# Attention with a gated memory part, ahead of two mixture stages: the memory's normalisation moved into column layout

## Chip, cores and metric

The kernel runs on one core of one Trainium2 chip. The metric is the device time of one execution in microseconds (us); times are compared as the median of several runs. TensorE multiplies matrices into PSUM banks, VectorE (DVE), ScalarE (ACT) and GpSimd (POOL) work elementwise, and SyncE (SP) issues most transfers.

## What is computed

The change lies in the first stage, an attention over 4 x 8 heads of 576 tokens and 64 features. Its output is a gated sum of a causal softmax attention and of a lookup in a memory matrix, which is divided by a norm. Two mixture stages follow, which the change doesn't touch.

```python
def _attn_ref(q, k, v, M_prev, z_prev, beta):
    scores = scale * np.matmul(q, k.transpose(0, 1, 3, 2))   # causal mask, softmax -> a
    local = np.matmul(a, v)
    def phi(x):
        return np.where(x > 0, x, np.exp(x) - 1.0) + 1.0
    q_p = phi(q)
    mem_ret = np.einsum('bhsd,bhde->bhse', q_p, M_prev)
    mem_norm = np.einsum('bhsd,bhd->bhs', q_p, z_prev)[..., None] + 1e-06
    mem_out = mem_ret / mem_norm
    g = 1.0 / (1.0 + np.exp(-beta))[None, :, None, None]
    return g * mem_out + (1 - g) * local
```

All of it is in float32. The host lays q and k out with features on partitions, two heads (a pair) stacked to 128 partitions; M of a pair is block diagonal, 128 x 128, and the two columns behind it hold z, each in its head's rows.

## The kernel before

The order of the work on every engine is the order in which the code is written; the tools add the waits. There are 16 pairs of heads (n), and each has four units (u): the first covers 256 query tokens, two cover 128 each, the last covers 64. The main loop runs over the 64 units, t = 4n + u. In step t it issues, in this order: the scores of unit t+3 (`scores`, L311 and L318, for a last unit L340 and L341), the rest of the softmax of unit t+1, the product with the values of unit t-1 (`av`, L399 and L404), the transposes of unit t (`transp`, L364, for a last unit L372 and L374), the exponentials of unit t+3, and what `later` has booked for step t (`run_late`). `scores` leaves a row maximum from DVE (L322, L343), exponentials from ACT (L327, L345), and on POOL a multiplication by the reciprocal of the sum and by 1-g (L337, L351); the reciprocals are DVE's (L331, L349). The transposed probabilities go from PSUM to SBUF on ACT and DVE (L367, L369).

The memory part is `phi_part`, a generator that is advanced one piece at a time. For pair m the pieces are booked in the steps of the pair before it: in the first step ACT's exponential of q (L267) and POOL's gate on M (L268; L270 copies the two z columns behind it into the same tile mg); in the second DVE's features (L272, L273, tile phi, two buffers); in the third and fourth the lookup. There TensorE takes 128 tokens of the features as weights and moves mg with its 130 columns (L279, three matmuls, then two), with tokens on partitions in `bank[6]`; DVE adds 1e-6 to the two norm columns, takes the reciprocal (L282, L283) and multiplies the rest by it into mem (L284). In `av` that result is brought into column layout, with features on partitions, by a matmul with mem as weights and the identity as the moving operand (L404), which adds to the sums of L399 in `bank[7]`. ACT copies them to xT (L85, `put_x`).

During the attention DVE, ACT and POOL also convert weights of the first mixture stage (`convert`, L237 to L246, transfers L221 and L224, the tile cst), and in steps 39 to 60 split its first inputs (L448 on DVE, L449 on POOL). For the loads of later pairs SP waits until the buffer of two pairs before is read: qr and mr (M and z) have two buffers each.

Of the kernel before, what the change touches and what calls it, by code (L numbers as in the profile page):

```python
# [9 lines left out]
F32 = mybir.dt.float32  # L10
# [7 lines left out]
ALU = mybir.AluOpType  # L18
# [3 lines left out]
P = 128  # L22
# [9 lines left out]
def kernel(ctx, tc, qt, kt, vt, mt, beta, w_in, w_out,  # L32
                           w_gate, w_noise, noise, w1, w2, out):

    nc = tc.nc
    NPAIR, _, S = kt.shape
    H, D = beta.shape[0], 64
    B = 2 * NPAIR // H
    NT = B * S
    NB = (S + P - 1) // P  # L40
    TAIL = S - (NB - 1) * P
    HS = S // 2
    QW, MW = qt.shape[-1], mt.shape[-1]
# [8 lines left out]
    bank = [two[i // 2][:, i % 2, :] for i in range(4)] + [psp.tile([P, 512], F32, name=f"bk{i}") for i in range(4, 8)]  # L52
# [7 lines left out]
    ident = const.tile([P, P], F32, name="ident")  # L60
# [48 lines left out]
    def consts():  # L109
        nc.gpsimd.memset(padr, 0.0)  # L110
        nc.gpsimd.iota(padr[:, :, P], pattern=[[P, CAP // P]], base=NT, channel_multiplier=1,
                       allow_small_or_imprecise_dtypes=True)
        yield
        nc.gpsimd.memset(tri, 1.0)
        nc.gpsimd.affine_select(out=tri, in_=tri, pattern=[[1, P]], compare_op=ALU.is_gt,
                                fill=0.0, base=0, channel_multiplier=-1)
        nc.gpsimd.memset(onesb, 1.0)
        yield
        for t, pat, m in ((iota8, [[1, NE]], 0), (runs, [[STRIDE, NE]], 0), (pid, [[0, 1]], 1), (tokid, [[P, NOISE_T]], 1)):
            nc.gpsimd.iota(t, pattern=pat, base=0, channel_multiplier=m, allow_small_or_imprecise_dtypes=True)  # L120
        yield
        nc.gpsimd.memset(wgt, 0.0)
        for j, src in enumerate((w_gate, w_noise)):
            nc.sync.dma_start(wgt[:, :, j * NE:(j + 1) * NE], _ap(src, 0, [[NE, P], [P * NE, NCC], [1, NE]]))
        nc.sync.dma_start(noise_sb, _ap(noise, 0, [[NE, P], [P * NE, NOISE_T], [1, NE]]))
        yield
# [123 lines left out]
        i = 4 * fc + 2 * which  # L250
        return U[i], U[i + 1]

    qs, mem, mg, PB, PT = {}, {}, {}, {}, {}

    def scaled(n):

# [3 lines left out]
    def phi_part(n):  # L260

        qq = qr_[n % 2][:, :S]
        e = ap2.tile([P, S], F32, name="phe", bufs=1)
        ph = ap2.tile([P, S], F32, name="phi", bufs=2)
        mg = ap2.tile([P, MW], F32, name="mg", bufs=1)
        mem[n] = ap2.tile([P, NB, P], F32, name="mem")
        nc.scalar.activation(e, qq, AF.Exp)  # L267
        nc.gpsimd.tensor_scalar(mg[:, :P], mr_[n % 2][:, :P], gtc[:, n % (H // 2):n % (H // 2) + 1], 1.0,  # L268
                                op0=ALU.mult, op1=ALU.mult)
        nc.gpsimd.tensor_copy(mg[:, P:], mr_[n % 2][:, P:])  # L270
        yield
        nc.vector.tensor_scalar_min(e, e, 1.0)  # L272
        nc.vector.scalar_tensor_tensor(ph, qq, 0.0, e, op0=ALU.max, op1=ALU.add)  # L273
        yield
        for ts in ((0, 1, 2), (3, 4)):
            k_ = len(ts)
            for i, t in enumerate(ts):
                w = min(P, S - t * P)
                nc.tensor.matmul(bank[6][:w, i * MW:(i + 1) * MW], ph[:, t * P:t * P + w], mg, start=True, stop=True)  # L279
            r = bank[6][:, :k_ * MW].rearrange("p (t c) -> p t c", c=MW)  # L280
            rd = ap2.tile([P, 3, 2], F32, name="rd")[:, :k_, :]
            nc.vector.tensor_scalar_add(rd, r[:, :, P:], 1e-6)  # L282
            nc.vector.reciprocal(rd, rd)  # L283
            nc.vector.tensor_tensor(mem[n][:, ts[0]:ts[0] + k_, :].rearrange("p t (j d) -> p t j d", j=2),  # L284
                                    r[:, :, :P].rearrange("p t (j d) -> p t j d", j=2),
                                    rd[:, :, :, None].to_broadcast([P, k_, 2, D]), op=ALU.mult)
            yield

    LEAD = 3
# [64 lines left out]
    def transp(t):  # L354
        n, u = units[t]
        pb = PB.pop(t)
        pt = ap3.tile([P, 2 * 512], F32, name="PT", bufs=2)
        PT[t] = pt
        if u < NK - 1:
            m = sum(w for _, w, _ in tiles(u))  # L360
            blocks = [(0, 0), (1, 1), (2, 2)] if u == 0 else [(c, c) for c in range(u + 2)]
            for j in range(2):
                for c, x in blocks:
                    nc.tensor.transpose(bank[4 + j][:, x * P:(x + 1) * P], pb[:, j * 512 + c * P:j * 512 + (c + 1) * P], ident)  # L364
                dst = pt[:, j * 512:j * 512 + m]
                if j == 0:
                    nc.scalar.activation(dst, bank[4][:, :m], AF.Copy)  # L367
                else:
                    nc.vector.tensor_copy(dst, bank[5][:, :m])  # L369
        else:  # L370
            for c in range(4):
                nc.tensor.transpose(bank[4][:, c * P:(c + 1) * P], pb[:, c * P:(c + 1) * P], ident)  # L372
            nc.scalar.activation(pt[:, :512], bank[4], AF.Copy)
            nc.tensor.transpose(bank[5][:TAIL, :P], pb[:, 4 * P:S], ident)  # L374
            nc.vector.tensor_copy(pt[:TAIL, 512:512 + P], bank[5][:TAIL, :P])

    def av(t):
        n, u = units[t]
        b, hp = n // (H // 2), n % (H // 2)
        vv = vr_[n % 2].rearrange("p (c j d) -> p c j d", c=NB, j=2)  # L380
        pt = PT.pop(t)
        q0 = (u + 1) * P if u else 0
        if u == 0:
            w = 2 * P
            work = [(0, P, 0, 0, w), (1, P, w, P, w)]
            rows = [(0, 0), (1, P)]
        elif u < NK - 1:
            w = P
            work = [(c, P, c * P, 0, w) for c in range(u + 2)]
            rows = [(u + 1, 0)]  # L390
        else:
            w = TAIL
            work = [(c, P, c * P, 0, w) for c in range(4)] + [(4, TAIL, 512, 0, w)]
            rows = [(u + 1, 0)]
        o = bank[7][:, :w]
        step = TAIL if u == NK - 1 else 512
        for i, (c, k_, x, a, e) in enumerate(work):
            for j in range(2):
                nc.tensor.matmul(o[j * D:(j + 1) * D, a:e], vv[:k_, c, j, :], pt[:k_, j * step + x:j * step + x + e - a],  # L399
                                 start=i == 0, stop=False, skip_group_check=True)  # L400
        for i, (qi, a) in enumerate(rows):
            k_ = min(P, w)
            for j in range(2):
                nc.tensor.matmul(o[j * D:(j + 1) * D, a:a + k_], mem[n][:k_, qi, j * D:(j + 1) * D], ident[:k_, :k_],  # L404
                                 start=False, stop=i + 1 == len(rows), skip_group_check=True)
        put_x(hp, b * S + q0, o)

    NU = len(units)
    CONV0, CONVR, CONVM = 3, 4.1, 1.9
    late = {}  # L410

    def later(step, gen):
        late.setdefault(max(step, -1), []).append(gen)
# [5 lines left out]
    for m in range(1, NPAIR):  # L419
        later(NK * (m - 1) - 1, first(m))  # L420
        gen = phi_part(m)
        for k_ in range(4):
            later(NK * (m - 1) + k_, gen)
    gen = consts()
    for k_ in range(4):
        later(k_, gen)
# [64 lines left out]
    for t in range(NU):  # L491
        n, j = divmod(t, NK)
        ahead = t + LEAD < NU
        if ahead:
            sg[t + LEAD] = scores(t + LEAD)
            next(sg[t + LEAD])
            next(sg[t + LEAD])
        for _ in sg.pop(t + 1, ()):
            pass
        if t:  # L500
            av(t - 1)
        else:
            next(phi0)
        transp(t)
        if t + 2 in sg:
            next(sg[t + 2])
        for g in range(2):
            cs = [c for c in range(NCC) if early[g][c] == t]
            if cs:
                hb = p1(g, 0, g, cs)  # L510
            if NCC - 1 in cs:
                act = act1(hb, True)
                ahead_of[g] = next(act)
                next(act)
        if ahead:
            next(sg[t + LEAD])
        if not t:
            next(phi0)
        run_late(t)
        d, m = divmod(t - 39, 3)  # L520
        if m == 0 and 0 <= d < 2 * NCC:
            split_x(d // NCC, d % NCC, nc.gpsimd, nc.vector.tensor_copy)
        if j == 0:
            next(fill, None)
        if j == 1 and n + 1 < NPAIR and n:
            load(n + 1, (vr_,))
        if j == 0 and not n:
            load(2, (qr_, mr_))
        if j == 2:
            if n + 2 < NPAIR:  # L530
                load(n + 2, (kr_,))
            if n + 3 < NPAIR:
                load(n + 3, (qr_, mr_))
# [539 lines left out]
```

## Time and profile before

| | |
|---|---|
| median of 3 runs | 1130.9 us (1129.4 to 1130.94) |
| profiled execution | 1130.14 us, span 1128.4 us |
| TensorE matmul busy | 1101.8 us (98%), 7182 instructions |
| weight loads busy | 956.0 us (85%) |
| DVE, ACT, POOL busy | 590.6, 513.3, 241.1 us |

The page divides the span into 40 slices of 28.2 us; the attention takes a little over the first eight. TensorE's busy time is modelled from pipelined instructions, and a full row does not mean that the array moves columns all the time. The weight loads (PEld) run beside the matmuls, in the same order, and their start times tell when the engine came to a block. In the forms, 128\*64 means 128 rows and 64 columns of the array.

### The profile page before, as it was taken

How to read it: one execution, taken by the hardware profiler on the slowest of the kernel's cores; microseconds unless marked ns; L12 is line 12 of the kernel's file. 1: busy time of each engine (PE TensorE's matmuls, PEld its weight loads, DVE VectorE, ACT ScalarE, POOL GpSimd, SP SyncE). 2: the span in 40 equal slices, each digit the busy share in tenths (PEclk: the TensorE clock that was granted, in tenths of full speed). 3: DMA queues.
4: the chain of work that ended last, by engine and by line, in shares of the span. 5: the costliest groups of instructions: out<-in, count | busy, mean ns of one | idle time of the engine just before them, and what ended most of it. 6: DMA issues, size and time to landing. Idle time of an engine off the chain costs nothing. (4 is left out here: it accounts for less than half of the span.)

```text
span 1128.4 us, 18965 instructions
## 1 busy us (share of the span) xinstructions
PE 1101.8 (98%) x7182; PEld 956.0 (85%) x7182; DVE 590.6 (52%) x1480; ACT 513.3 (45%) x1202; POOL 241.1 (21%) x359
## 2 busy tenths in 40 slices
PE   7999999999999999999999999899999999999995
PEld 5777777789999888898989888799999999999994
DVE  5787877669995445434347644444444444432211
ACT  5777777657665334334245533333333333331211
POOL 5566566600000022200202012102020202020202
PEclk9999999999999999999999999999999999999998
DMA  6996432034330011100125507535454535441213
GB/s 191 279 270 210 160 105 85 18 99 130 119 118 16 2 57 57 48 10 11 57 56 163 155 29 207 147 117 124 114 127 112 128 115 125 113 91 35 28 19 46
DMA packets 98278, 115.47 MB, mean 102 GB/s; under 512 B 9984, under 2 KB 67328, under 8 KB 98176
## 3 DMA queue, kind: packets, MB, share of 16 engines
q1 hardware_dynamic: 89664, 94.42, 27.9%
q0 software_dynamic: 8512, 19.74, 8.8%
q8 instruction: 58, 0.95, 0.4%
q14 instruction: 44, 0.36, 0.1%
HBM read 77.80 MB, written 36.33 MB: 101 GB/s over the span
## 5 line engine op out<-in xcount | busy, mean ns | idle before, releaser
L459 PE MATMUL bk<-xsplit,u 128*128 128x384 f32 x1152 | 220.2, 339 | 2.0 <-ACT hact L470 2.0
L547 PE MATMUL bk<-u,hsplit 128*128 128x512 f32 x864 | 215.2, 393 | 0.0
L756 PE MATMUL bk<-u,hsplit 128*128 128x512 f32 x802 | 214.0, 391 | 0.2 <-DVEq L907 0.2
L459 PEld LDWEIGHTS bk<-xsplit,u 128*128 128x128 f32 x1152 | 202.4, 188 | 12.0 <-ACT hact L470 2.7
L547 PEld LDWEIGHTS bk<-u,hsplit 128*128 128x128 f32 x864 | 160.7, 188 | 29.3
L756 PEld LDWEIGHTS bk<-u,hsplit 128*128 128x128 f32 x802 | 147.4, 188 | 27.4 <-DVEq L907 0.4
L747 ACT ACTIVATE hsplit<-bk 128x312 fp32r<-128x312 f32 (+2 forms) x126 | 54.5, 432 | 235.4 <-PE bk L743 205.2
L743 PE MATMUL bk<-xsplit,u 128*128 128x312 f32 (+1 forms) x864 | 135.0, 311 | 3.6 <-ACTq L907 3.1
L743 PEld LDWEIGHTS bk<-xsplit,u 128*128 128x128 f32 x864 | 128.3, 188 | 6.6 <-ACTq L907 3.6
L678 POOL DMA_INDIRECT xs<-x,si x36 | 38.4, 1066 | 413.8 <-DVE runs L671 175.9
L470 ACT ACTIVATE hact<-bk 128x384 f32<-128x384 f32 x96 | 47.0, 489 | 155.1 <-PE bk L459 155.0
L767 POOL DMA_INDIRECT out_dram<-xT,tk x30 | 47.5, 1584 | 276.6 <-ACT xT L764 269.6
L475 DVE TENSOR_TENSOR hact<-hact 128x384 f32<-128x384 f32 x64 | 35.7, 558 | 125.7 <-ACT hsplit L471 125.6
L748 DVE SCALAR_TENSOR_TENSOR hsplit<-bk,hsplit 128x312 fp32r<-128x312 f32 (+2 forms) x68 | 33.2, 488 | 113.2 <-ACT hsplit L747 113.2
L579 DVE TENSOR_TENSOR u<-xT,u 128x512 fp32r<-128x512 f32 x89 | 60.9, 691 | 52.4 <-ACT u L578 51.5
L743 PE MATMUL bk<-x2b,u 128*128 128x312 f32 x576 | 87.5, 308 | 0.0
L337 POOL TENSOR_SCALAR P<-P,sm,omg 128x128 f32<-128x128 f32 (+3 forms) x128 | 77.3, 616 | 36.1 <-DVE rd L282 27.4
L743 PEld LDWEIGHTS bk<-x2b,u 128*128 128x128 f32 x576 | 83.4, 189 | 0.7
L578 ACT ACTIVATE u<-xT 128x512 fp32r<-128x512 f32 x89 | 55.6, 628 | 54.5 <-PE bk L756 50.4
L748 DVE SCALAR_TENSOR_TENSOR xsplit<-bk,hsplit 128x312 fp32r<-128x312 f32 (+1 forms) x58 | 27.8, 478 | 89.3 <-ACT hsplit L747 89.3
L327 ACT ACTIVATE P<-bk,mx 128x128 f32<-128x128 f32 (+3 forms) x128 | 65.9, 528 | 14.0 <-DVE mx L322 13.7
L399 PE MATMUL bk<-PT,vr 128*64 128x128 f32 (+3 forms) x896 | 61.6, 271 | 0.4 <-ACT PT L367 0.3
(186 smaller groups left out, 1464.9 us busy)
## 6 DMA issues: line engine op xcount, KB each, us to landing
xT<-in_moe_w_dram SPq DMA_DIRECT2D x89, 256.0 KB, 3.2
cst<-in_moe_w_in_dram SPq DMA_DIRECT2D x32, 256.0 KB, 2.8
cst<-in_moe_w_out_dram SPq DMA_DIRECT2D x32, 256.0 KB, 2.9
xs<-zero SPq DMA_DIRECT2D x5, 1536.0 KB, 10.0
out_dram<-zero SPq DMA_DIRECT2D x4, 1472.0 KB, 7.6
qr<-in_q_dram SPq DMA_DIRECT2D x16, 352.0 KB, 3.1
xr<-xs SPq DMA_DIRECT2D x7, 774.0 KB, 4.7
vr<-in_v_dram SPq DMA_DIRECT2D x16, 320.0 KB, 3.5
```

What stands on the lines that cost most here:

```text
L327: nc.scalar.activation(pb[:, j * 512 + o:j * 512 + o + w], sp[:, j, o:o + w], AF.Exp, bias=mx[:, x:x + 1], scale=-1.0, accum_out=sm[:, x:x ...
L337: nc.gpsimd.tensor_scalar(v, v, sm[:, x:x + 1], omg[:, h0 + j:h0 + j + 1], op0=ALU.mult, op1=ALU.mult)
L399: nc.tensor.matmul(o[j * D:(j + 1) * D, a:e], vv[:k_, c, j, :], pt[:k_, j * step + x:j * step + x + e - a], start=i == 0, stop=False, skip ...
L459: nc.tensor.matmul(hb, l[:, sl], r, start=cc == 0 and n == 0, stop=cc == NCC - 1 and n == 2)
L547: nc.tensor.matmul(bank[y0 + t], l[:, sl], r, start=fc == 0 and n == 0, stop=fc == NFC - 1 and n == 2)
L578: nc.scalar.activation(hi, st, AF.Copy)
L579: eng.tensor_sub(lo, st, hi.bitcast(F32))
L743: nc.tensor.matmul(bank[bk][:, :n_], l[:, cs], r[:, cc, sl], start=cc == 0 and n == 0, stop=cc == NCC - 1 and n == 2)
L747: nc.scalar.activation(hh[:, sl], bank[bk][:, :n_], AF.Relu)
L748: nc.vector.scalar_tensor_tensor(hl[:, sl], bank[bk][:, :n_], 0.0, hh[:, sl].bitcast(F32), op0=ALU.max, op1=ALU.subtract)
L756: nc.tensor.matmul(bank[self.ybank + t], l[:, sl], r, start=fc == 0 and n == 0, stop=fc == NFE - 1 and n == 2)
L767: add = nc.gpsimd.indirect_dma_start(out=out, out_offset=bass.IndirectOffsetOnAxis(ap=self.tok[:n, t:t + 1], axis=0), in_=y, in_offset=Non ...
```

## The change

The norm is now taken out of the features, not out of the result. For each block of 128 tokens (the last block is shifted to start at token 448, so that it has 128 too), TensorE multiplies the features with the two z columns alone, straight from mr (L278 in the new numbering); DVE adds 1e-6 and takes the reciprocal of all ten columns at once (rd). Then rd, one column of it repeated 64 times as the weights, is multiplied with the identity: this brings the reciprocals into column layout, repeated over the 64 feature rows of each head (L288, three token blocks, then two). DVE multiplies the features by it in place (L291). `av` no longer uses mem: it multiplies mg, now only the gated M (128 x 128, block diagonal), with the divided features, one matmul per head and unit (L404). POOL's copy of z falls away.

```diff
@@ phi_part
+        mg[n] = ap2.tile([P, P], F32, name="mg")
+        phd[n] = ph
         nc.scalar.activation(e, qq, AF.Exp)
-        nc.gpsimd.tensor_copy(mg[:, P:], mr_[n % 2][:, P:])
         yield
         nc.vector.tensor_scalar_min(e, e, 1.0)
         nc.vector.scalar_tensor_tensor(ph, qq, 0.0, e, op0=ALU.max, op1=ALU.add)
         yield
+        at = [min(t * P, S - P) for t in range(NB)]
+        dn = bank[6][:, :2 * NB]
+        for t in range(NB):
+            nc.tensor.matmul(dn[:, 2 * t:2 * t + 2], ph[:, at[t]:at[t] + P], mr_[n % 2][:, P:], start=True, stop=True)
+        rd = ap2.tile([P, NB, 2], F32, name="rd")
+        nc.vector.tensor_scalar_add(rd, dn.rearrange("p (t j) -> p t j", j=2), 1e-6)
+        nc.vector.reciprocal(rd, rd)
+        yield
         for ts in ((0, 1, 2), (3, 4)):
+            a, e_ = ts[0] * P, min(S, (ts[-1] + 1) * P)
+            for t in ts:
                 w = min(P, S - t * P)
-                nc.tensor.matmul(bank[6][:w, i * MW:(i + 1) * MW], ph[:, t * P:t * P + w], mg, start=True, stop=True)
-            nc.vector.tensor_scalar_add(rd, r[:, :, P:], 1e-6)
-            nc.vector.reciprocal(rd, rd)
-            nc.vector.tensor_tensor(mem[n]..., r[:, :, :P]..., rd..., op=ALU.mult)
+                for j in range(2):
+                    nc.tensor.matmul(bank[6][j * D:(j + 1) * D, t * P - a:t * P - a + w], rd[:, t, j:j + 1].to_broadcast([P, D]),
+                                     ident[:, P - w:], start=True, stop=True)
+            yield
+            nc.vector.tensor_tensor(ph[:, a:e_], ph[:, a:e_], bank[6][:, :e_ - a], op=ALU.mult)
             yield
@@ av
-        for i, (qi, a) in enumerate(rows):
-            k_ = min(P, w)
-            for j in range(2):
-                nc.tensor.matmul(o[j * D:(j + 1) * D, a:a + k_], mem[n][:k_, qi, j * D:(j + 1) * D], ident[:k_, :k_],
-                                 start=False, stop=i + 1 == len(rows), skip_group_check=True)
+        for j in range(2):
+            nc.tensor.matmul(o[j * D:(j + 1) * D, :], mg[n][:, j * D:(j + 1) * D], phd[n][:, q0:q0 + w],
+                             start=False, stop=True, skip_group_check=True)
@@ booking and main loop
-        for k_ in range(4):
+        for k_ in range(5):
             later(NK * (m - 1) + k_, gen)
+        for k_ in (3, 4):
+            between[NK * (m - 1) + k_] = gen
@@ in step t, behind av(t - 1)
+        if t in between:
+            next(between[t])
         transp(t)
...
-        if not t:
+        if t < 2:
+            next(phi0)
             next(phi0)
```

On TensorE, third unit of a pair, between the transposes and the next scores, the row L279 before:

```order
L364 MATMUL bk_64<-ident,P 128x128 x4
L279 MATMUL bk_65<-mg,phi 128x130 x3
L311 MATMUL bk_61<-kr_137,qs 128x512 x2
```

and now:

```order
L369 MATMUL bk_64<-ident,P 128x128 x4
L278 MATMUL bk_65<-mr_141,phi 128x2 x5
L316 MATMUL bk_61<-kr_137,qs 128x512 x2
```

The five sums of the pair stand where three of its lookups stood. On TensorE from the fourth unit to the next pair's first transposes, before (bk_65 is `bank[6]`, bk_66 is `bank[7]`):

```order
L404 MATMUL bk_66<-ident,mem 64x128 x2
L372 MATMUL bk_63<-ident,P 128x128 x4
L374 MATMUL bk_64<-ident,P 64x128
L279 MATMUL bk_65<-mg,phi 128x130
L279 MATMUL bk_65<-mg,phi 64x130
L340 MATMUL bk_62<-kr_137,qs 128x288 x2
L341 LDWEIGHTS identb
L341 MATMUL bk_62<-maskt,identb 128x64
L399 MATMUL bk_66<-PT,vr_138 64x64 x10
L404 MATMUL bk_66<-ident,mem 64x64 x2
L364 MATMUL bk_63<-ident,P 128x128 x3
```

and now:

```order
L404 MATMUL bk_66<-phi,mg 64x128 x2
L288 MATMUL bk_65<-ident,rd 64x128 x6
L377 MATMUL bk_63<-ident,P 128x128 x4
L379 MATMUL bk_64<-ident,P 64x128
L345 MATMUL bk_62<-kr_137,qs 128x288 x2
L346 LDWEIGHTS identb
L346 MATMUL bk_62<-maskt,identb 128x64
L401 MATMUL bk_66<-PT,vr_138 64x64 x10
L404 MATMUL bk_66<-phi,mg 64x64 x2
L288 MATMUL bk_65<-ident,rd 64x128 x2
L288 MATMUL bk_65<-ident,rd 64x64 x2
L369 MATMUL bk_63<-ident,P 128x128 x3
```

The broadcasts stand behind L404, ahead of the transposes; the lookups behind the transposes are gone. On DVE over the same stretch, before:

```order
L322 TENSOR_REDUCE mx<-bk_61 128x2
L375 COPY PT<-bk_64 64x128
L331 RECIPROCAL sm<-sm 128x2
L282 TENSOR_SCALAR rd<-bk_65 128x4
L283 RECIPROCAL rd<-rd 128x4
L284 TENSOR_TENSOR mem<-bk_65,rd 128x256
L343 TENSOR_REDUCE mx<-bk_62 128x1
L369 COPY PT<-bk_64 128x384
L331 RECIPROCAL sm<-sm 128x2
L322 TENSOR_REDUCE mx<-bk_61 128x2 x2
```

and now:

```order
L327 TENSOR_REDUCE mx<-bk_61 128x2
L380 COPY PT<-bk_64 64x128
L336 RECIPROCAL sm<-sm 128x2
L291 TENSOR_TENSOR phi<-phi,bk_65 128x384
L348 TENSOR_REDUCE mx<-bk_62 128x1
L374 COPY PT<-bk_64 128x384
L336 RECIPROCAL sm<-sm 128x2
L291 TENSOR_TENSOR phi<-phi,bk_65 128x192
L327 TENSOR_REDUCE mx<-bk_61 128x2 x2
```

The wide product stands in the fourth unit, where three instructions on two blocks stood, and the narrow one in the next pair's first unit, ahead of the reduction.

## Rows read from the trace of the kernel before

**Rows 1.** The page: TensorE's busy time, and the granted clock in 40 slices.

```profile
PE 1101.8 (98%) x7182; PEld 956.0 (85%) x7182; DVE 590.6 (52%) x1480; ACT 513.3 (45%) x1202; POOL 241.1 (21%) x359
...
PEclk9999999999999999999999999999999999999998
```

**Rows 2.** Busy us by stretch, one pair each: PE, PEld, DVE, ACT, POOL, clock, DMA.

```profile
28.56:42.06 13.50, 13.50 (x146) 10.07 (x145) 10.24 (x23) 9.72 (x30) 7.27 (x15) 1.00 0.97 234
...
149.95:163.43 13.48, 13.48 (x145) 10.04 (x144) 11.00 (x28) 9.90 (x31) 7.44 (x13) 1.00 0.32 100
163.43:177.66 14.23, 14.12 (x145) 10.31 (x144) 9.69 (x24) 10.06 (x32) 11.20 (x23) 1.00 0.31 94
...
191.31:205.46 14.15, 13.76 (x145) 10.09 (x144) 10.88 (x26) 9.97 (x32) 8.19 (x16) 1.00 0.14 45
```

**Rows 3.** Weight loads in order of time, one pair: start, us, line, tiles, array, form, count.

```profile
103.67 0.25 PEld L404 LDWEIGHTS bk<-ident,mem 128*64 128x64 f32 x4
104.09 0.86 PEld L364 LDWEIGHTS bk<-ident,P 128*128 128x128 f32 x8 [0.17 <-POOL P L351]
104.92 0.75 PEld L279 LDWEIGHTS bk<-mg,phi 128*128 128x128 f32 x6
105.79 0.30 PEld L311 LDWEIGHTS bk<-kr,qs 64*128 64x128 f32 x4
...
108.70 0.61 PEld L279 LDWEIGHTS bk<-mg,phi 128*128 128x128 f32 x4
109.49 0.78 PEld L340 LDWEIGHTS bk<-kr,qs 128*128 128x128 f32 x4 [0.17 <-issue]
...
111.41 0.20 PEld L404 LDWEIGHTS bk<-ident,mem 64*64 64x64 f32 x4
111.68 0.64 PEld L364 LDWEIGHTS bk<-ident,P 128*128 128x128 f32 x6
...
114.15 0.47 PEld L404 LDWEIGHTS bk<-ident,mem 128*64 128x64 f32 x8
114.79 0.64 PEld L364 LDWEIGHTS bk<-ident,P 128*128 128x128 f32 x6 [0.17 <-issue]
```

**Rows 4.** The same view, narrow: first two loads of L372, second load of L340.

```profile
108.20 0.20 PEld L372 LDWEIGHTS bk<-ident,P 128*128 128x128 f32 x2 [0.17 <-issue]
...
109.59 0.19 PEld L340 LDWEIGHTS bk<-kr,qs 128*128 128x128 f32 x1
```

**Rows 5.** All engines in order of time, at the start of the attention.

```profile
14.35 0.80 DVE L273 SCALAR_TENSOR_TENSOR phi<-qr,phe 128x576 f32<-128x576 f32 x1
...
15.27 0.74 PEld L279 LDWEIGHTS bk<-mg,phi 128*128 128x128 f32 x6 [1.77 <-POOL mg L270]
```

**Rows 6.** DVE in order of time, third and fourth unit of the pair.

```profile
106.36 0.56 DVE L284 TENSOR_TENSOR mem<-bk,rd 128x384 f32<-128x384 f32 x1
...
110.23 0.15 DVE L331 RECIPROCAL sm<-sm 128x2 f32<-128x2 f32 x1
...
110.68 0.42 DVE L284 TENSOR_TENSOR mem<-bk,rd 128x256 f32<-128x256 f32 x1
```

**Rows 7.** SP's queue and POOL in order of time, the same pair.

```profile
104.99 0.58 SPq L143 DMA_DIRECT2D mr<-in_M_prev_dram  x1
105.62 0.42 SPq L224 DMA_DIRECT2D cst<-in_moe_w_out_dram  x1
...
112.23 0.37 POOL L268 TENSOR_SCALAR mg<-mr,gtc 128x128 f32<-128x128 f32 x1
```

**Rows 8.** Order of time, late pairs: idle time of the engine and what ended it, in brackets.

```profile
166.18 0.17 DVE L331 RECIPROCAL sm<-sm 128x2 f32<-128x2 f32 x1 [2.00 <-POOL sm L330]
...
168.26 0.20 PEld L399 LDWEIGHTS bk<-PT,vr 128*64 128x64 f32 x4 [0.56 <-DVE PT L369]
...
200.90 0.52 PEld L279 LDWEIGHTS bk<-mg,phi 128*128 128x128 f32 x4 [0.63 <-DVE phi L273]
```

More of the change, by code (lines that the diff above doesn't have):

```diff
@@ L251, in wu @@
         return U[i], U[i + 1]
-    qs, mem, mg, PB, PT = {}, {}, {}, {}, {}
+    qs, mg, phd, PB, PT = {}, {}, {}, {}, {}
     def scaled(n):
@@ L264, in phi_part @@
         ph = ap2.tile([P, S], F32, name="phi", bufs=2)
-        mg = ap2.tile([P, MW], F32, name="mg", bufs=1)
-        mem[n] = ap2.tile([P, NB, P], F32, name="mem")
+        mg[n] = ap2.tile([P, P], F32, name="mg")
+        phd[n] = ph
         nc.scalar.activation(e, qq, AF.Exp)
-        nc.gpsimd.tensor_scalar(mg[:, :P], mr_[n % 2][:, :P], gtc[:, n % (H // 2):n % (H // 2) + 1], 1.0,
+        nc.gpsimd.tensor_scalar(mg[n], mr_[n % 2][:, :P], gtc[:, n % (H // 2):n % (H // 2) + 1], 1.0,
                                 op0=ALU.mult, op1=ALU.mult)
-        nc.gpsimd.tensor_copy(mg[:, P:], mr_[n % 2][:, P:])
         yield
@@ L274, in phi_part @@
         yield
+        at = [min(t * P, S - P) for t in range(NB)]
[6 more added lines that the diff above has]
+        yield
         for ts in ((0, 1, 2), (3, 4)):
-            k_ = len(ts)
-            for i, t in enumerate(ts):
+            a, e_ = ts[0] * P, min(S, (ts[-1] + 1) * P)
+            for t in ts:
                 w = min(P, S - t * P)
-                nc.tensor.matmul(bank[6][:w, i * MW:(i + 1) * MW], ph[:, t * P:t * P + w], mg, start=True, stop=True)
-            r = bank[6][:, :k_ * MW].rearrange("p (t c) -> p t c", c=MW)
-            rd = ap2.tile([P, 3, 2], F32, name="rd")[:, :k_, :]
-            nc.vector.tensor_scalar_add(rd, r[:, :, P:], 1e-6)
-            nc.vector.reciprocal(rd, rd)
-            nc.vector.tensor_tensor(mem[n][:, ts[0]:ts[0] + k_, :].rearrange("p t (j d) -> p t j d", j=2),
-                                    r[:, :, :P].rearrange("p t (j d) -> p t j d", j=2),
-                                    rd[:, :, :, None].to_broadcast([P, k_, 2, D]), op=ALU.mult)
+                for j in range(2):
[3 more added lines that the diff above has]
+            nc.vector.tensor_tensor(ph[:, a:e_], ph[:, a:e_], bank[6][:, :e_ - a], op=ALU.mult)
             yield
@@ L385, in av @@
             work = [(0, P, 0, 0, w), (1, P, w, P, w)]
-            rows = [(0, 0), (1, P)]
         elif u < NK - 1:
@@ L389, in av @@
             work = [(c, P, c * P, 0, w) for c in range(u + 2)]
-            rows = [(u + 1, 0)]
         else:
@@ L393, in av @@
             work = [(c, P, c * P, 0, w) for c in range(4)] + [(4, TAIL, 512, 0, w)]
-            rows = [(u + 1, 0)]
         o = bank[7][:, :w]
@@ L409 @@
     CONV0, CONVR, CONVM = 3, 4.1, 1.9
-    late = {}
+    late, between = {}, {}
     def later(step, gen):
```

## Prediction

> **What bounds the kernel now.** I read the page's first part and its clock line first: TensorE is busy 98% of the span and its granted clock is high in all slices [rows 1]. The change touches only the attention, which ends near 236 us, so the next view is the busy time of each engine in stretches cut at the same place of each head pair (the first weight load of L340, the scores of a pair's last unit). The ten pairs from 28.56 to 163.43 us take 134.87 us, 13.49 each; the first and the last of them take 13.50 and 13.48 with DVE busy 10.2 to 11.0, ACT 9.7 to 9.9 and POOL 7.3 to 7.4 us of it [rows 2]. Two later pairs, with extra work on POOL, take 14.23 and 14.15 [rows 2]. Equal periods, with no other engine near full, say that TensorE's own instructions set the time. The third view checks that: weight loads in order of time over one pair [rows 3]. A full busy row proves little, since ends are modelled; so I take the price of a block from its start to the next block's start. Each f32 matmul of the code shows as two instructions there (three L279 as x6).
>
> **The price list.** L364 x8 takes 104.09 to 104.92, 0.10 per instruction. L404 x4 takes 0.42 (103.67 to 104.09) and x8 0.64 (114.15 to 114.79) [rows 3]: four more instructions cost 0.22. As the two heads' 64-column halves run side by side, a pair of instructions with 128 moving columns costs 0.11, and 0.20 is left at the block's end, where the next instruction uses the array in another shape (128\*64 to 128\*128). With 64 moving columns, L404 x4 takes 0.27 [rows 3], 0.055 per pair of instructions and 0.16 for the end. L279 x6 takes 0.87 (104.92 to 105.79), 0.11 each and 0.21 for the end, before the 64-row scores; L279 x4, with a change of shape inside and one behind, 0.79 (108.70 to 109.49) [rows 3].
> The row shows 0.2 us at such a border. The Trainium skill, TensorEngine Tiling (Array Packing), Tiling Modes, says that changing the tiling mode, though not merely the tile, drains the engine. By it the borders must be counted as well as the columns, and the trace agrees (0.42 against two times 0.11); priced by columns alone the sum would come out at the third rival's time below.
>
> **The change, part by part, per pair of heads.** The steps are the four units of a pair.
> (1) Sums, third unit: five matmuls with the features as weights and two moving columns take the place of the three of L279. Ten loads; does one of 128 f32 columns still cost 0.11? The nearest row is L340, whose second load starts 0.10 after the first, before any long matmul lies between [rows 4]; lower bound, the transposes, whose first two loads start 0.06 apart (both, 0.14 each, lie within 0.20) [rows 4]. I take 0.11, as L340 and L279 are plain f32 loads. The tail keeps the drain but not the 0.11 of moving columns: 0.10. Sum 10 x 0.11 + 0.10 = 1.20 for 0.87: +0.33.
> (2) First broadcast, fourth unit: six matmuls, twelve instructions in the shape of L404, which they follow without a border: 6 x 0.11 = +0.65 (unrounded 0.109).
> (3) L279 x4 falls away, and with it two borders, since transposes and L340 have one shape: -0.79.
> (4) Next pair's first step: L404's 64-column block was 0.27 [rows 3]. Now the products with mg need 128 rows behind the 64-row tail of L399: one more border (0.10, the part of 0.16 beyond 0.055, and an exposed first load of 0.05), then 2 x 0.055 for mg, 2 x 0.11 and 2 x 0.055 for the second broadcast, and 0.16 at the end: 0.75. +0.47 (unrounded 0.74).
> (5) The 256-column product of the first unit is one pair of matmuls instead of two of 128: two instructions of 0.21 for four of 0.11: -0.02.
> The sum is 0.33 + 0.65 - 0.79 + 0.47 - 0.02 = +0.64, fifteen times: +9.6 us. The first pair is outside the loop. There L279 waits until 15.27, in name for the copy L270, but the features of L273 end only at 15.15 [rows 5], so dropping the copy gives nothing; the first broadcast follows the transposes, where L279's second block had waited for DVE, and I call that even (-0.1); the second broadcast stands alone between transposes and scores: 0.33 and one border, +0.48. Last unit: a border, +0.1. Together +0.5.
>
> **What other engines do with it.** DVE loses 0.56 (L284, 384 wide) from the third unit and does that product in the fourth, where L282 to L284 went; the 192-wide one, about 0.35 (an estimate on the line through 0.56 for 384 and 0.42 for 256 columns), is new in the next step [rows 6]. L331 there starts at 110.23, so the first product would end near 111.0, and TensorE reaches the second broadcast near 111.85 (L404's 111.41, +0.19 from items 1 to 3, +0.25 from item 4): some 0.7 us of cover, and without it the wait is TensorE's. POOL loses the copy L270, 0.19. L268 (mg) now waits for the last products of the pair two before; on TensorE these end near 111.7, and it starts at 112.23 [rows 7]. The load of M into mr now waits for the sums instead of POOL: SP issues it at 104.99, the weights' cst behind it at 105.62 [rows 7]; both would go about 1.2 us later, and M is wanted by POOL six steps on, near 20 us. Nothing.
> One wait that TensorE has now, 0.63 for the features at 200.90 [rows 8], should be covered by the longer steps: -0.6. In the pair from 163.43, L331 starts 2.00 late behind POOL, and TensorE waits 0.56 for L369 [rows 8]; there the product of DVE stands behind that L331, ends near 166.9, and the second broadcast would wait about 1 us. That takes over the old wait and adds some 0.4. Net -0.2.
> The stages behind 236 us start later by the whole sum; their own transfers are set off by the end of the attention, so I see nothing that gives it back.
> **Sum:** +9.6 + 0.5 - 0.2 = +9.9 on the profiled execution of 1130.14 us (span 1128.4 and 1.7 around it), 1140.0. That execution is 0.76 under the median 1130.9 and inside the spread of 1.5; adding half of that gives 1140.4.
>
> **Rivals.**
> *Not slower:* the sums are nearly free. If the ten loads cost 0.06 as for transposes, item 1 falls by 0.5 and the total to about +2 (1132); if the price goes by moving columns and the loads hide, two of 128 are 0.002, the block is its end alone, item 1 falls by 1.1, and the pair is 0.46 shorter: -6.6, 1123.5. It ends on the other side once a load costs under 0.045 us (0.64 regained over ten). Speaking for it: the transposes [rows 4]; against: L340 and L279, the same type and width, at 0.10 to 0.11. Chance 5%. The same page of the Trainium skill, Performance Considerations, gives a matmul of one moving column the latency of one with 60; by that floor, an estimate of 0.025 us each, the time would be about 1127. No row here shows such a matmul.
> *A new wait in every pair:* the chain sums, reciprocal, broadcast, product, broadcast runs through DVE's queue. If the product ends over 0.7 us later than I think, the second broadcast waits each time; 0.5 us of it gives +7.5, 1148. For it: L331 and the reductions share the queue, and one pair shows it. Against: DVE idles 2.5 us per pair [rows 2]. 10%.
> *The borders don't go:* if dropping L279 x4 saves only its columns, 0.44 of instructions instead of 0.79, the pair costs about 0.95 more: +14.5 in all, 1145. 7%.
>
> **How the numbers follow.** My forecast has 78%, with its own range 1138 to 1143: 0.1 us per pair either way is 1.5, the waits 0.8, the run itself 0.8. To leave out no more than 2 in 10 the range reaches to the third rival and part of the second: 1137.2 to 1145.2. Within 0.2% (2.3 us, about what a measurement of this kernel can tell from no change) lies only the first rival's upper part: same 3%, faster 2%, slower 95%.
>
> **What would show it.** The pair's period from L340's counterpart to the next goes from 13.49 to 14.1; a block of ten loads with two moving columns takes 1.2; no gap stands ahead of the second broadcast, except near 166 us; DVE is busy 0.4 less per pair, POOL 0.2. I am wrong if the loads come closer than 0.1 us, if a wait for DVE shows in every pair, or if the stages behind the attention are not simply moved.

## The result, and the profile after

The changed kernel takes 1142.93 us (median of 4 runs, 1141.99 to 1144.37) against 1130.92 for the kernel before (4 runs, 1129.4 to 1131.32): a ratio of 1.0106 (95% interval [1.0093, 1.0118]), some 12.0 us slower. The forecast was 1140.4, in a range from 1137.2 to 1145.2. The profiled execution took 1141.99 (span 1140.3). The first part of the page and its clock line answer to [rows 1]: TensorE has 256 more instructions and is as full as before.

```profile
PE 1115.4 (98%) x7438; PEld 971.5 (85%) x7438; DVE 585.9 (51%) x1448; ACT 512.5 (45%) x1202; POOL 239.2 (21%) x343
...
PEclk9999999999999999999999999999999999999998
```

Busy time by stretch, in the columns of [rows 2], cut at the first weight load of L345 (L340 before): the first and the last of the ten pairs without extra work on POOL, and the first of the late ones.

```profile
30.27:44.45 14.18, 14.18 (x163) 10.86 (x161) 10.58 (x23) 9.60 (x29) 7.26 (x14) 1.00 0.98 231
157.86:172.04 14.18, 14.18 (x163) 10.86 (x162) 10.65 (x26) 9.90 (x30) 7.85 (x13) 1.00 0.30 94
172.04:186.63 14.59, 14.39 (x162) 10.94 (x160) 8.71 (x20) 9.89 (x30) 10.22 (x21) 1.00 0.30 92
```

The period is 14.18 for 13.49, +0.69 per pair, in all ten. The late pairs take 14.59, 14.37, 14.38 and 14.18: less of a wait above the period (0.41, 0.19, 0.20 and 0, in all 0.80) than before, where [rows 2] show 0.74 and 0.66 for two of them and the four together have 1.57. The blocks that changed stand in the weight loads of one pair in order of time, which answer to [rows 3]:

```profile
110.56 1.20 PEld L278 LDWEIGHTS bk<-mr,phi 128*128 128x128 f32 x10
111.77 0.30 PEld L316 LDWEIGHTS bk<-kr,qs 64*128 64x128 f32 x4
...
113.75 0.25 PEld L404 LDWEIGHTS bk<-phi,mg 128*64 128x64 f32 x4
113.97 0.69 PEld L288 LDWEIGHTS bk<-ident,rd 128*64 128x64 f32 x12
114.83 0.42 PEld L377 LDWEIGHTS bk<-ident,P 128*128 128x128 f32 x4 [0.17 <-issue]
115.22 0.11 PEld L379 LDWEIGHTS bk<-ident,P 128*64 128x64 f32 x1
115.33 0.79 PEld L345 LDWEIGHTS bk<-kr,qs 128*128 128x128 f32 x4
...
116.53 0.81 PEld L401 LDWEIGHTS bk<-PT,vr 128*64 128x64 f32 x20 [0.26 <-issue]
117.41 0.20 PEld L404 LDWEIGHTS bk<-phi,mg 128*64 128x64 f32 x4
117.52 0.42 PEld L288 LDWEIGHTS bk<-ident,rd 128*64 128x64 f32 x8
118.01 0.64 PEld L369 LDWEIGHTS bk<-ident,P 128*128 128x128 f32 x6
```

From start to start: the sums take 1.21 (110.56 to 111.77). L404 and the first broadcast take 1.08 (113.75 to 114.83), where L404 alone took 0.42. Behind L379 the scores L345 follow at once, at 115.33, with no lookup between. L404 and the second broadcast take 0.60 (117.41 to 118.01).

In one pair the second broadcast waits. All engines in order of time, with idle time and what ended it in brackets:

```profile
173.98 0.17 DVE L336 RECIPROCAL sm<-sm 128x2 f32<-128x2 f32 x1 [1.35 <-POOL sm L335]
...
174.06 0.53 DVE L291 TENSOR_TENSOR phi<-phi,bk 128x384 f32<-128x384 f32 x1
...
174.12 0.20 PEld L404 LDWEIGHTS bk<-phi,mg 128*64 128x64 f32 x4
...
174.65 0.41 PEld L288 LDWEIGHTS bk<-ident,rd 128*64 128x64 f32 x8 [0.34 <-DVE phi L291]
```

POOL is late, so L336 is, so is the product L291 behind it on DVE, and L288 starts 0.53 after L404 where it took 0.11 in the pair above: a wait of 0.42.

Where the 11.9 us between the two profiled spans came in, by the start times of the same TensorE block in both traces:

| stretch of TensorE (before) | after, us | before, us | difference | forecast |
|---|---|---|---|---|
| to the first L340 at 12.56 | 12.17 | 12.56 | -0.39 | 0 |
| from there to the next pair's, 28.56 | 18.10 | 16.00 | +2.10 | +0.6 |
| ten pairs, to 163.43 | 141.77 | 134.87 | +6.90 | +6.4 |
| four late pairs, to 218.96 | 57.52 | 55.53 | +1.99 | +2.4 |
| last pair, to the first mixture stage alone, 234.73 | 16.41 | 15.77 | +0.64 | +0.5 |
| to the gap between the stages, 721.83 | 486.55 | 487.10 | -0.55 | 0 |
| from there to the end | 407.78 | 406.57 | +1.21 | 0 |

The rows of the start and of the end hold for these two executions only: both kernels were profiled once more (below), and there the differences to the first L340, to the next pair's, over the ten and over the four late pairs are +1.96, +1.38, +6.90 and +2.01; from there to the gap, the last pair included, it is +0.6, and from the gap to the end +0.13.

### The profile page after: what moved, and what is told of

It reads as the page before. It is cut to its first block, busy times and chain, and to the rows that moved or that the text cites. A ratio compares the mean times of both kernels' runs of the same rounds, so it can differ in the third digit from the quotient of the medians.

```text
span 1140.3 us, 19456 instructions
## 1 busy us (share of the span) xinstructions
PE 1115.4 (98%) x7438; PEld 971.5 (85%) x7438; DVE 585.9 (51%) x1448; ACT 512.5 (45%) x1202; POOL 239.2 (21%) x343
## 5 line engine op out<-in xcount | busy, mean ns | idle before, releaser
L401 PE MATMUL bk<-PT,vr 128*64 128x128 f32 (+3 forms) x896 | 60.9, 271 | 0.3 <-ACT PT L372 0.3
```

## Experiments

The first four experiments, the one on the norm in column layout and the repetition of the kernel before are one execution each. What is read from them is mostly the period, which is the same from pair to pair, and the blocks within it.

### One matmul for all sums

A single matmul takes the place of the five; so four of the five blocks have no sums of their own.

```diff
-        for t in range(NB):
-            nc.tensor.matmul(dn[:, 2 * t:2 * t + 2], ph[:, at[t]:at[t] + P], mr_[n % 2][:, P:], start=True, stop=True)
+        nc.tensor.matmul(dn, ph[:, :P], mr_[n % 2][:, None, P:].to_broadcast([P, NB, 2]), start=True, stop=True)
```

> The changed kernel, but one matmul with the features of the first token block as weights gives all ten sums (ten moving columns, z repeated five times); the sums of the other four blocks are left out. Eight of ten weight loads go. If a load of 128 f32 columns costs 0.11 us whatever moves behind it, the block falls from 1.21 to about 0.33, the pair's period from 14.18 to 13.30, and the time by 15 x 0.88 = 13 us to about 1129. If the price goes by moving columns (ten in all, as before), the period stays 14.18 and the time near 1142.

Measured 1129.71 us, period 13.29. Its weight loads in order of time:

```profile
103.82 0.30 PEld L277 LDWEIGHTS bk<-mr,phi 128*128 128x128 f32 x2
104.14 0.30 PEld L315 LDWEIGHTS bk<-kr,qs 64*128 64x128 f32 x4
```

The block took 0.32 for 1.21: eight loads fewer give 0.89 back, 0.11 each. The sums are paid by their weights, and the rival by which they are nearly free falls.

### A hundred columns in each sum

```diff
-        dn = bank[6][:, :2 * NB]
+        dn = bank[6][:, :100 * NB]
...
-            nc.tensor.matmul(dn[:, 2 * t:2 * t + 2], ph[:, at[t]:at[t] + P], mr_[n % 2][:, P:], start=True, stop=True)
+            nc.tensor.matmul(dn[:, 100 * t:100 * t + 100], ph[:, at[t]:at[t] + P], mr_[n % 2][:, MW - 100:], start=True, stop=True)
...
-        nc.vector.tensor_scalar_add(rd, dn.rearrange("p (t j) -> p t j", j=2), 1e-6)
+        nc.vector.tensor_scalar_add(rd, dn.rearrange("p (t j) -> p t j", j=100)[:, :, 98:], 1e-6)
```

> The changed kernel, but each of the five sums moves 100 columns of mr (98 of M, then the two of z) in place of two. If loads set the block's price, the columns hide behind the next load and only the last matmul's show: +0.08 per pair, period 14.26, about 1143. If the price goes by moving columns, each of ten instructions gains 98/128 of 0.11: +0.84 per pair, period 15.0, near 1155.

Measured 1143.97, period 14.26. The same view:

```profile
111.41 1.20 PEld L278 LDWEIGHTS bk<-mr,phi 128*128 128x128 f32 x10
112.70 0.30 PEld L316 LDWEIGHTS bk<-kr,qs 64*128 64x128 f32 x4
```

Fifty times the moving columns cost 0.08 per block (1.29 for 1.21), presumably the last matmul's own run into the border. Up to 100 columns hide behind a load of 128.

### The broadcasts behind the transposes

```diff
+        transp(t)
         if t in between:
             next(between[t])
-        transp(t)
```

The same instructions, with three changes of the array's shape more per pair.

> The changed kernel, but the broadcasts stand behind the transposes in place of ahead of them, so that three more changes of the array's shape come in each pair (transposes to broadcast twice, broadcast to L345's 128 rows and columns once); the same instructions otherwise. If a change of shape costs 0.15 to 0.2 us, the period is 14.65 to 14.8 and the time 1149 to 1151. If the borders cost nothing and only columns and loads count, 14.18 and 1142. If waits behind DVE are the danger, gaps appear ahead of the second broadcast, since the first product comes 0.5 us later.

Measured 1149.01, period 14.67, +0.49. The fourth unit and the next pair's first:

```profile
102.54 0.25 PEld L404 LDWEIGHTS bk<-phi,mg 128*64 128x64 f32 x4
102.97 0.42 PEld L377 LDWEIGHTS bk<-ident,P 128*128 128x128 f32 x4 [0.17 <-POOL P L342]
103.35 0.11 PEld L379 LDWEIGHTS bk<-ident,P 128*64 128x64 f32 x1
103.66 0.63 PEld L288 LDWEIGHTS bk<-ident,rd 128*64 128x64 f32 x12 [0.20 <-issue]
104.47 0.78 PEld L345 LDWEIGHTS bk<-kr,qs 128*128 128x128 f32 x4 [0.17 <-ACT PT L378]
...
106.54 0.20 PEld L404 LDWEIGHTS bk<-phi,mg 128*64 128x64 f32 x4
106.81 0.64 PEld L369 LDWEIGHTS bk<-ident,P 128*128 128x128 f32 x6
```

L404 takes 0.43 for 0.22, L379 0.31 for 0.11, the second L404 0.27 for 0.11, and the first broadcast 0.05 less. The tags in brackets name POOL, ACT or "issue" for these gaps, yet they have the size of the borders of [rows 3], and come and go with the order of the blocks, the instructions being the same. What does not count is the printed shape alone: L379 is printed as 128\*64 and stands between blocks of 128\*128 without a border in the changed kernel (0.11), but has one here (0.31) ahead of L288, which is printed as 128\*64 too. The transposes thus go with the 128\*128 blocks, as item 3 took them. No wait for DVE shows ahead of the second broadcast. A border costs 0.16 on average, and 0.2 where 128 columns run before it. The Trainium skill, TensorEngine Tiling (Array Packing), Tiling Modes, says that a change of the mode drains the engine; these rows agree, and give the price; that the 0.16 is a drain is the page's word, the rows show the time only.

### The memory products ahead of the 64-row tail

In a pair's last unit the products with mg stood behind the value product of the last 64 rows, which has another shape.

```diff
+            if k_ < P:
+                memory()
...
-        for j in range(2):
-            nc.tensor.matmul(o[j * D:(j + 1) * D, :], mg[n][:, j * D:(j + 1) * D], phd[n][:, q0:q0 + w],
-                             start=False, stop=True, skip_group_check=True)
+        if u < NK - 1:
+            memory()
```

> The changed kernel, but in the last unit of a pair the products with mg stand ahead of the 64-row tail of the values, so that the way back from 64 rows to 128 joins the one to the broadcast only: one border stays between tail and broadcast, so if my item 4 put the border at the right place nothing is gained in the steady pairs (period 14.18, 1142) but the last unit gets shorter by 0.1; if instead the border belongs to the change of operands (mg behind values), the pair gains 0.15 (14.03, 1139.6).

Measured 1142.55, period 14.18. The weight loads of that step (L408 is `av`'s value product here, L401 the product with mg):

```profile
117.45 0.55 PEld L408 LDWEIGHTS bk<-PT,vr 128*64 128x64 f32 x16 [0.26 <-issue]
117.91 0.20 PEld L401 LDWEIGHTS bk<-phi,mg 128*64 128x64 f32 x4
118.18 0.20 PEld L408 LDWEIGHTS bk<-PT,vr 64*64 64x64 f32 x4
118.44 0.41 PEld L288 LDWEIGHTS bk<-ident,rd 128*64 128x64 f32 x8
```

The four blocks take 1.47 (to 118.92) for the 1.48 of after (116.53 to 118.01). The border is only moved, since the second broadcast behind the tail needs 128 rows again.

### The start: a filled wait, and both kernels once more

The first pair was 1.5 dearer than forecast. Weight loads of after in order of time:

```profile
14.80 1.19 PEld L278 LDWEIGHTS bk<-mr,phi 128*128 128x128 f32 x10 [1.69 <-DVE phi L272]
15.83 0.98 PEld L369 LDWEIGHTS bk<-ident,P 128*128 128x128 f32 x6
17.14 1.15 PEld L288 LDWEIGHTS bk<-ident,rd 128*64 128x64 f32 x12 [0.33 <-issue]
18.62 0.93 PEld L316 LDWEIGHTS bk<-kr,qs 64*128 64x128 f32 x8 [0.33 <-ACT phe L267]
```

Its stretches of 2 us, with the granted clock third from the end:

```profile
16.00:18.00 2.00, 2.00 (x15) 1.67 (x16) 1.01 (x4) 1.39 (x4) 1.71 (x6) 0.56 0.00 0
18.00:20.00 2.00, 2.00 (x20) 1.42 (x16) 0.56 (x1) 0.39 (x1) 1.86 (x4) 0.59 0.52 162
```

The clock is near its lower level (1.2 of 2.4 GHz) from 16 to 20 us, behind a wait of 1.69 for the features that ended at 14.80. The kernel before waits 1.77 at this place [rows 5], and its clock was 1.00 throughout. Three runs ask whether this belongs to the change: one fills the wait with matmuls whose result nobody reads, the other two repeat both kernels unchanged.

```diff
+            for _ in range(6):
+                nc.tensor.matmul(bank[7][:, :P], ident, ident, start=True, stop=True)
             next(phi0)
```

> The changed kernel with six matmuls of the identity with itself, whose result nothing reads, put into the wait ahead of the first sums (1.4 us in the profile). If the 1.5 us that the start lost beyond my sum is TensorE's clock, which stood at 0.56 to 0.59 from 16 to 20 us after that wait, the clock stays at 1.00 there, the stretch from the first sums to the next scores falls from 3.8 to about 2.7 us, and the time by 1.5 us, to about 1141. If it is waits for DVE in the first chain, the stretch stays and the time is that of the changed kernel, 1143 or a little more.

> The changed kernel once more, beside the others of this call: the steady pairs at 14.18 again, since nothing in them waits; start and the place near 732 us may differ by the clock, 1.5 us each. 1142 to 1144.5.

> The kernel before once more, for its clock: if the lower clock at the start belongs to the change (two moving columns in place of 130), it stays at 1.00 from 16 to 20 us here; if it belongs to the wait that both kernels have, some executions of this kernel show it as well. Steady pairs at 13.49.

Filled: 1141.95 (4 runs, 1140.78 to 1143.4), ratio 1.0100 [1.0085, 1.0116]. The changed kernel again: 1143.1 (4 runs, 1142.61 to 1144.17), 1.0110 [1.0094, 1.0125]. The intervals overlap, so in time this is inconclusive. The kernel before again took 1131.23 (one execution). The steady pairs take 14.18, 14.18 and 13.49 as before. Two stretches of the kernel before (12 to 14 us reads 0.50 too):

```profile
14.00:16.00 2.00, 1.74 (x8) 1.77 (x9) 0.99 (x4) 1.02 (x3) 1.61 (x4) 0.50 0.00 0
16.00:18.00 2.00, 2.00 (x10) 1.57 (x8) 1.48 (x5) 1.42 (x4) 0.24 (x2) 0.50 0.00 0
```

So the low clock there comes to the kernel before as well, in some executions. It was low ahead of the wait already, which in that run lasted 1.19 and ended at 14.23; so the wait is not shown to be the cause. The three blocks from the first lookup to the scores took 4.10 there (14.23 to 18.33) for 2.79 in the first profile (15.27 to 18.06). The changed kernel's three (sums, transposes, broadcast) took 3.82 in the first trace (14.80 to 18.62) and 5.08 in the repetition; with the wait filled, 2.73:

```profile
17.11 1.20 PEld L278 LDWEIGHTS bk<-mr,phi 128*128 128x128 f32 x10
...
19.84 0.52 PEld L316 LDWEIGHTS bk<-kr,qs 64*128 64x128 f32 x8 [0.17 <-issue]
```

In that run low clock had come and gone earlier: the four loads of L345 ahead of the filling took 1.60 for 0.84. So it doesn't show that the filling keeps the clock up.

The three blocks are thus as good as even at full clock (2.73 for 2.79), as forecast, and the excess goes with the clock: at low clock the changed kernel pays about 1 us more than the old one (5.08 against 4.10, one execution each). Part of this is that the old 2.79 holds a wait of 0.66 for DVE, ahead of L279's second block, which shrank to 0.20 when TensorE was slow; the new blocks are work nearly throughout. In the repetition of the changed kernel and in the run with the filling the row of the granted clock reads 1.00 from 12 to 20 us, although L278 took 1.94 in the first of them for its 1.21 and L345 1.60 in the second; low clock is inferred there, from stretched blocks of fixed work.

### The kernel before without its own border

If borders cost what they seem to, the kernel before has two to save per pair: the lookup of the last 64 tokens sits in another shape. Here that block is shifted to start at token 448, as the change does, and the memory products, which now have 128 rows, go ahead of the 64-row tail.

```diff
-                w = min(P, S - t * P)
-                nc.tensor.matmul(bank[6][:w, i * MW:(i + 1) * MW], ph[:, t * P:t * P + w], mg, start=True, stop=True)
+                x = min(t * P, S - P)
+                nc.tensor.matmul(bank[6][:, i * MW:(i + 1) * MW], ph[:, x:x + P], mg, start=True, stop=True)
...
+                    nc.tensor.matmul(o[j * D:(j + 1) * D, a:a + min(P, w)], mem[n][:, qi, j * D:(j + 1) * D], ident[:, P - min(P, w):],
```

> The kernel before with one idea of the change: the last token block of the lookup is shifted to start at token 448, so that its weights have 128 columns, and in the last unit the products with mem stand ahead of the 64-row tail. Two changes of the array's shape go (128 to 64 columns inside L279's second block and back to L340's 128), the instructions stay. If borders are the credit that my item 3 counted, the second block falls from 0.79 to 0.44, the pair's period from 13.49 to about 13.14, and the time by 5 to 6 us, to about 1125. If borders cost nothing, 1130.5.

Measured 1129.84 (11 runs, 1127.4 to 1131.24), ratio 0.9988 [0.9979, 0.9997], 1.0 us gained where 5 to 6 were expected; period 13.39 for 13.49. Weight loads, and a line of the view of waits over 41 to 161 us (us in total, times, longest):

```profile
107.75 0.53 PEld L279 LDWEIGHTS bk<-mg,phi 128*128 128x128 f32 x4
108.19 0.79 PEld L340 LDWEIGHTS bk<-kr,qs 128*128 128x128 f32 x4
...
111.43 0.52 PEld L311 LDWEIGHTS bk<-kr,qs 64*128 64x128 f32 x8 [0.40 <-ACT qs L258]
```

```profile
PEld bk L311 <- ACT qs L258: 3.6, 9, 0.4
```

The lookup takes 0.44 for the 0.79 of [rows 3]: the borders go as item 3 had it. But 0.24 of it comes back 3.2 us later, where the next pair's scores now wait 0.40 in place of 0.16, for ACT's scaled q (L258).

### The same, with ACT's work one step earlier

```diff
-        later(NK * (m - 1) - 1, first(m))
+        later(NK * (m - 1) - 2, first(m))
```

> The kernel before without the border, as in the run on that, and ACT's scaling of q for the next pair (L258) one unit earlier. In that run the scores of the next pair's first unit waited 0.4 us for L258 instead of the usual 0.16, and the period stayed at 13.39. If that wait alone gave the border's gain back, the period is now 13.15 and the time 5 us under that of the kernel before, about 1126. If the next limit (DVE's queue, 10.9 us busy per pair and late by its conversions) is as near, the period stays above 13.3 and the time near 1130.

Measured 1128.23 (9 runs, 1125.03 to 1129.34) against 1131.33 (13 runs), ratio 0.9969 [0.9959, 0.9979]: 0.3% under the kernel before, and so under the changed one. The first two stretches of one pair:

```profile
27.69:40.84 13.15, 13.15 (x146) 10.02 (x145) 10.11 (x25) 9.73 (x30) 7.27 (x15) 1.00 0.93 209
40.84:54.75 13.91, 13.22 (x146) 10.10 (x145) 10.93 (x26) 10.03 (x31) 8.01 (x16) 1.00 1.08 307
```

The period is the expected 13.15, so L258 was the wait. The gain is 3.1 and not 5: one pair loses 0.76 in a wait at 44.57, for which the trace names ACT's copy L367 in one row and the load of kr in another (L367 had ended at 44.18, so the load is the likelier; not settled); the late pairs keep their waits; and in the profiled execution the 3.6 gained by the attention's end (231.12 for 234.73) shrank to 1.8 in the span (1126.6), since 24 matmuls behind the gap between the stages took 6.26 for 3.71, at a granted clock of 0.55 (the kernel before took 5.24 for them when it was repeated, see below).

### The norm in column layout from the start

Without sums in rows and broadcasts: z's column, repeated 64 times, is the weights, and the features move through it (384 and 192 columns); DVE then adds, takes the reciprocal and multiplies on full width.

```diff
+            for j in range(2):
+                nc.tensor.matmul(nm[j * D:(j + 1) * D, :], mr_[n % 2][:, P + j:P + j + 1].to_broadcast([P, D]), ph[:, a:e_],
+                                 start=True, stop=True)
...
+            nc.vector.tensor_scalar_add(rd, nm, 1e-6)
+            nc.vector.reciprocal(rd, rd)
+            nc.vector.tensor_tensor(ph[:, a:e_], ph[:, a:e_], rd, op=ALU.mult)
```

> Another way to the norm in column layout, without sums per token and without the broadcast: a z column repeated 64 times as weights, the features moving (384, then 192 columns), behind the products of units three and four; then DVE adds 1e-6, takes the reciprocal of all 576 columns and multiplies. TensorE would need 13.49 - 0.87 - 0.79 + 0.96 + 0.15 = 12.9 us per pair. If DVE's reciprocal takes one element per cycle like its other operations, the period is near 13 and the time 1122 to 1125. But the small reciprocals of the trace grow from 0.164 us for 4 elements to 0.303 for 24, 7 ns each: 576 would take 4 us, DVE would be busy about 15 us per pair and set the period, and the time would be 1150 to 1156.

Measured 1199.12, 68 us above the kernel before. Groups on DVE by shape, 30 to 200 us (count, busy us, mean ns):

```profile
L283 DVE RECIPROCAL rd<-rd 128x384 f32<-128x384 f32 x10 | 25.5, 2553 | 0.3
L283 DVE RECIPROCAL rd<-rd 128x192 f32<-128x192 f32 x10 | 13.5, 1353 | 0.3
```

The price of the reciprocal, 3.9 us per pair, was as expected; the loss was not, at over 4 us per pair with DVE 73% to 83% busy from 60 to 120 us. All engines in order of time show how:

```profile
66.77 2.55 DVE L283 RECIPROCAL rd<-rd 128x384 f32<-128x384 f32 x1
...
72.42 0.27 DVE L373 COPY PT<-bk 64x128 f32<-64x128 f32 x1
...
72.75 0.19 PEld L394 LDWEIGHTS bk<-PT,vr 64*64 64x64 f32 x4 [2.36 <-DVE PT L373]
```

L373, which TensorE needs at once, stands in DVE's queue behind the long reciprocal and what that held up, and TensorE waits 2.36. From 30 to 230 us there are eleven such waits for L373, 21.7 us in all. The stretch behind that wait:

```profile
74.00:80.00 6.00, 5.54 (x30) 3.32 (x29) 2.99 (x7) 3.31 (x9) 2.56 (x6) 0.50 0.42 109
```

For the next 6 us the granted clock is 0.50. Waits and the clock together make up the loss; how much belongs to each was not separated, and this is one execution.

## Why the prediction was right, point by point

- **What bounds it:** TensorE's own instructions did set the pair's time. The period moved by the sum of the block prices in all ten pairs, with DVE, ACT and POOL idle for 3.5 us and more of each.
- **Items 1 to 5:** the sums came to 1.21 (1.20 forecast); the first broadcast added 0.66 (0.65); the lookup's 0.79 is gone; the next pair's first step adds 0.48 (0.47): L401, L404 and the second broadcast take 0.88, 0.11 and 0.49 where L399 and L404 had taken 1.00. The 256-column product takes 0.64 before and after (-0.02 forecast). That is 0.34 + 0.66 - 0.79 + 0.48 = +0.69 for +0.64, the 0.05 being the sum of these small differences; over fifteen pairs 0.7 us.
- **Sums nearly free:** refuted, 0.11 per load (one matmul for all sums). The floor that the Trainium skill gives on its page TensorEngine Tiling (Array Packing), Performance Considerations, for short matmuls (0.025 us as an estimate) is not what a short f32 matmul with 128 columns of its own weights costs here: two instructions of 0.11.
- **Borders don't go:** refuted, in the changed kernel and by the shortened lookup in the kernel before (0.44 for 0.79).
- **A new wait in every pair:** did not come. The one new wait is where it was forecast, behind POOL's late step, but 0.42 at 174 and not about 1: product and L404 both came later, and the old wait of 0.74 at this pair went with it.
- **The waits, a term mis-sized:** -0.2 forecast, -0.8 measured (0.80 in the four late pairs for 1.57).
- **The start, the term that was furthest off:** +0.6 with the first pair's share of the items; up to the next pair's L340 +1.7 was measured (-0.39 and +2.10), and +3.3 in the repetitions (+1.96 and +1.38). The work was priced well (2.73 for 2.79 when the clock is full); the low clock at the start was not thought of. It comes to both kernels, so a part of these two numbers is chance.
- **Signs on other engines:** over the whole span DVE is 4.7 us less busy and POOL 1.9, which is 0.29 and 0.12 per pair where 0.4 and 0.2 were forecast. Nothing in the time hangs on it.
- **The stages behind "start later by the whole sum":** off by +0.66 in the first two profiles (-0.55 up to the gap, +1.21 behind it), but this is the clock of one execution. Matmuls in order of time behind the gap, for the changed kernel, the kernel before, and the kernel before once more:

```profile
732.52 5.25 PE L748 MATMUL bk<-xsplit,u 128*128 128x312 f32 x24 [3.36 <-ACTq L912]
```

```profile
721.83 3.71 PE L743 MATMUL bk<-xsplit,u 128*128 128x312 f32 x24 [3.14 <-ACTq L907]
```

```profile
721.52 5.24 PE L743 MATMUL bk<-xsplit,u 128*128 128x312 f32 x24 [3.18 <-ACTq L907]
```

The same 24 matmuls take 5.25 for 3.71, with a granted clock of 0.72 from 732 to 738 against 1.00 from 721 to 727. Repeated, the kernel before takes 5.24 for them, at 0.72 from 721 to 727, and from the gap to the end the repetitions differ by 0.13 (408.07 and 407.94). So the stages behind were simply moved, as forecast, and the first trace of the kernel before is the exception here.

- **The total:** the forecast difference of 9.5 in the medians became 12.0 (12.2 in the repetitions); 1142.93 is at the upper end of the forecast's own range, 1138 to 1143. The pairs account for some 9.5 of it (6.90 + 1.99 + 0.64), and the rest of 2.5 lies between the start's +1.7 and +3.3. That the forecast of these pairs (6.4 + 2.4 + 0.5 = 9.3) came out so near is partly luck, since the period's +0.7 over the fifteen pairs and the waits' -0.6 almost cancel.

## What to carry to other kernels

Price a short f32 matmul by its weight loads (two of 0.11 us per 128 columns here), and add 0.16 to 0.2 for each change of the array's shape; count the changes in the order of issue (here the transposes count with the 128\*128 blocks, also where only 64 columns are printed), since the same instructions in another order cost 0.49 per pair. A saving on the bounding engine is worth what the next wait leaves of it: 0.34 became 0.10 until ACT's step was moved up too. A wide reciprocal on VectorE costs its own time and that of whatever stands behind it in the queue.

## What the runs showed of the hardware

- The reciprocal on DVE takes 2.55 us for 384 f32 columns and 1.35 for 192, 6.3 ns per column; a product of two tensors of these widths takes 0.56 and 0.36, about 1 ns per column. The Trainium skill, VectorE: DVE Perf Modes, section Walkthrough: the 8-slice pipeline in each mode, describes the reciprocal as an iterative division that repeats 8 times; the runs show a ratio of about six per column, not how it comes about.
- The clock differs between executions of the same work: the kernel before had it at 1.00 around its wait of 1.77 at the start in one execution, and at 0.50 from 12 to 18 us in another; in the 6 us behind the gap between the stages (TensorE idle for 3.1 to 3.5 us) the first trace of the kernel before shows 1.00, the other eleven traces 0.50 to 0.76. Each such stretch costs TensorE 1 to 2.5 us. So one profile of each kernel can't settle a difference of that size at such a place.
